# Quarter sums of the weights on GpSimd alone, the single-tile group of the second channel product first, norms of two pairs at a time

## Chip, cores and metric

The kernel runs on one core of a Trainium2 chip. The metric is the device time of one execution in microseconds (us). A trace of one execution is taken by the hardware profiler; its span (first to last instruction) is about 2 us shorter than the time.

Engines: PE is TensorE's matmuls, PEld its weight loads, DVE is VectorE, ACT is ScalarE, POOL is GpSimd, SP is the engine that issues most transfers. "L507" is line 507 of that kernel's source. Lines shift between kernels: L561 of the kernel before is L564 of the changed one.

## The reference

Attention with RMS-normalised q and k, then an MLP-mixer (token mixing, then channel mixing) on its result. There are 8 batches, 12 heads, 448 positions, heads of 64, 768 channels, 256 and 1536 hidden units. All activations are float32; the four mixer weights come as float64.

```python
q_n, k_n = rmsnorm(q, g_q), rmsnorm(k, g_k)          # x / sqrt(mean(x*x) + 1e-6) * g
attn = softmax(q_n @ k_n.T / 8)                      # 448 x 448, per head
x = (attn @ v)                                       # put back to (B, 448, 768)
h = np.maximum(x.T @ w_tok1, 0.0) @ w_tok2           # 448 -> 256 -> 448
u = x + h.T
h2 = np.maximum(u @ w_ch1, 0.0) @ w_ch2              # 768 -> 1536 -> 768
return u + h2
```

## The kernel before

Both channel products are done with seven products of half-size blocks in place of eight (a Strassen scheme), so each needs sums of the weights' quarters. The float64 words of `w_ch1` and `w_ch2` come in as 36 chunks. Each chunk is converted to float32 by VectorE, ScalarE and GpSimd, four sums are made from its four quarters, and the eight blocks are stored to DRAM (`ws1`, `ws2`, `ws3`). PE later loads them back as "units", in every batch.

```python
def combine(j):                              # the four sums of chunk j, and its store
    w, group, m, t = stages[j]
    q = st.pop("stage")
    nc.vector.tensor_tensor(out=q[:, 4], in0=q[:, 1], in1=q[:, 3], op=ALU.add)
    nc.vector.tensor_tensor(out=q[:, 6], in0=q[:, 1], in1=q[:, 0], op=ALU.subtract)
    nc.gpsimd.tensor_tensor(out=q[:, 5], in0=q[:, 4], in1=q[:, 0], op=ALU.subtract)
    nc.gpsimd.tensor_tensor(out=q[:, 7], in0=q[:, 2], in1=q[:, 5], op=ALU.subtract)
    # ... cut: to = the block's place in ws1, ws2 or ws3
    nc.sync.dma_start(out=to.rearrange("q p n -> p q n"), in_=q[:])

def weight_items(lo, hi):                    # three chunks are in work at a time
    def one(i):
        convert_first(i)                     # VectorE: 3 operations
        convert_second(i - 1)                # ScalarE: 2
        convert_last(i - 2)                  # VectorE 1, GpSimd 1, then combine()
        weight_load(i + 2)                   # raw words, on the same queue as the store
```

(Range checks are cut there.) The chunks come in groups: 18 chunks of `w_ch1` (three groups of six), then `w_ch2`'s columns. PE can't use a group of `w_ch2` before all its chunks are stored.

```python
l += [(moe_w_ch2, 3, m, t) for t in range(KF) for m in range(2)]   # "double" group: chunks 19 to 30
l += [(moe_w_ch2, 4, 2, t) for t in range(KF)]                     # "single" group: chunks 31 to 36
```

The norms of a pair of heads: one square on ScalarE, one reduce on VectorE, then eleven small operations on VectorE (mean and epsilon, then the inverse root by three Newton steps). Slices are left out here.

```python
nc.scalar.activation(out=sq, in_=qk, func=AF.Square)
nc.vector.tensor_reduce(out=ms, in_=sq, axis=AX_X, op=ALU.add)
nc.vector.tensor_scalar(ms, ms, 1.0 / D, 1e-6, ALU.mult, ALU.add)
self.rsqrt(rs, ms)                            # ten operations on VectorE
```

A batch's program is a list that is merged with the next batch's attention. It begins with turns (transposes) of x and the first token product, and ends with the two groups of the second channel product and the turns of the result y:

```python
late = [(us(6, HS), lambda i=i, p=p: ch2(b, 0, i, p)) for i in range(7) for p in range(2)]
ys = [0, 1, KC, KC + 1]
for i in range(7):
    late.append((us(6, HS), lambda i=i: ch2(b, 1, i, 0)))
    if i and ys:
        late.append((0.5, lambda cc=ys.pop(0): trans_y(b, cc)))
late += [(0.5, lambda cc=cc: trans_y(b, cc)) for cc in (2, KC + 2)]
```

So four turns of y stand between products, and two stand at the very end, directly ahead of the next batch's three turns of x. I call that place the **seam**.

## Time and profile before

| | before |
|---|---|
| median of the first three runs | 1551.77 us (1550.86 to 1552.11) |
| span of the profiled run | 1550.2 us |
| busy: PE, VectorE, ScalarE, GpSimd | 1415.5, 761.6, 491.9, 468.1 us |
| mean granted TensorE clock | 0.966 |
| first token product of batch 1 | 383.5 us |
| from there to the last batch's first token product | 1039.9 us (five steps of 174.5 us, the last 167.6) |
| from there to the end | 126.8 us |

### The profile page before, as it was taken

The numbers are of one execution on the slowest core, as the hardware profiler recorded it, in microseconds if no ns is written. First come the engines' busy times: TensorE is split into PE (matmuls) and PEld (weight loads), VectorE is DVE, ScalarE is ACT, GpSimd is POOL, SyncE is SP. The second block draws the span as 40 slices with busy tenths as digits, with TensorE's granted clock in tenths as the row PEclk, the third lists the DMA queues.
The fourth block names the chain that finished last, engine by engine and source line by source line (L and its number), as shares of the span: only waits on it lengthen the run. The fifth ranks groups of instructions, "written<-read, shape, count | busy, mean of one in ns | idle before, by whom it ended". The sixth has DMA issues, their size and how long they took to land.

```text
span 1550.2 us, 19250 instructions
## 1 busy us (share of the span) xinstructions
PE 1415.5 (91%) x6976; PEld 1054.6 (68%) x6976; DVE 761.6 (49%) x1513; ACT 491.9 (32%) x850; POOL 468.1 (30%) x424
## 2 busy tenths in 40 slices
PE   5778668477999999999999999999999999999998
PEld 2233445377578857777578857777578857787898
DVE  6977777751454435543454435543454435422321
ACT  5645334311333232323333232323333232312110
POOL 2444455541233213331233213331233213320231
PEclk9989877789999999999999999999999999999999
DMA  5346777676145533446145434446145433444354
GB/s 128 102 138 190 215 207 225 191 242 187 45 140 159 148 87 112 147 132 176 45 140 159 147 87 111 146 131 177 45 140 157 148 88 110 132 125 127 112 166 138
DMA packets 229259, 217.11 MB, mean 140 GB/s; under 512 B 98116, under 2 KB 185668, under 8 KB 229156
## 3 DMA queue, kind: packets, MB, share of 16 engines
q1 hardware_dynamic: 205634, 204.55, 45.8%
q10 hardware_dynamic: 23522, 11.24, 2.7%
q8 instruction: 58, 0.95, 0.3%
q14 instruction: 45, 0.37, 0.1%
HBM read 185.86 MB, written 29.88 MB: 139 GB/s over the span
## 4 chain that ended last, share of the span: by engine, by line
PE 76%; DVE 12%; POOL 3%; issue 3%; ACT 2%; DMA 1%; ACTq 1%; POOLq 0%; SPq 0%; DVEq 0%
PE m_ps L561 24%; PE m_ps L503 22%; PE o_ps L326 8%; PE s_ps L269 8%; PE m_ps L425 5%; PE m_ps L433 4%; POOL stage L212 3%; PE d_ps L340 2%; PE t_ps L404 2%; DVE raw L183 2%; PE t_ps L254 2%; DVE e_t L210 2%; DVE es L316 1%; DVE e_t L182 1%; DVE ms L728 1%
## 5 line engine op out<-in xcount | busy, mean ns | idle before, releaser
L561 PE MATMUL m_ps<-hb,unit 128*128 128x224 f32 x2016 | 402.1, 357 | 30.2 <-DMA unit<-ws 30.2
L561 PEld LDWEIGHTS m_ps<-hb,unit 128*128 128x128 f32 x2016 | 379.9, 192 | 49.8 <-DMA unit<-ws 31.3
L275 ACT ACTIVATE e<-s_ps,rs 112x448 f32<-112x448 f32 x384 | 212.1, 634 | 207.0 <-PE s_ps L269 202.6
L503 PE MATMUL m_ps<-tu,unit 128*128 128x224 f32 x1152 | 238.0, 361 | 12.7 <-DVE hb L508 12.7
L503 PEld LDWEIGHTS m_ps<-tu,unit 128*128 128x128 f32 x1152 | 220.8, 195 | 26.9 <-DVE hb L508 13.1
L269 PE MATMUL s_ps<-qkT 64*112 64x448 f32 x768 | 180.9, 584 | 21.4 <-ACT qkT L256 18.1
L503 PE MATMUL m_ps<-uT,unit 128*128 128x224 f32 x864 | 178.0, 358 | 7.8 <-DVE uT L438 7.8
L503 PEld LDWEIGHTS m_ps<-uT,unit 128*128 128x128 f32 x864 | 161.7, 191 | 26.2 <-issue 11.6
L326 PE MATMUL o_ps<-e,vt 112*64 112x448 f32 x768 | 166.0, 553 | 1.8 <-DVE uT L358 1.8
L570 POOL TENSOR_TENSOR uT<-uT,r 128x448 f32<-128x448 f32 (+1 forms) x64 | 58.4, 923 | 286.3 <-DVE r L570 169.1
L312 POOL TENSOR_TENSOR es<-e 112x896 f32<-112x896 f32 x48 | 100.7, 2098 | 136.3 <-PE d_ps L340 136.3
L269 PEld LDWEIGHTS s_ps<-qkT 64*112 64x112 f32 x768 | 65.5, 181 | 100.0 <-issue 70.4
L316 DVE TENSOR_TENSOR es<-es,e 112x896 f32<-112x896 f32 x96 | 127.8, 1331 | 4.9 <-DVE es L316 0.5
L326 PEld LDWEIGHTS o_ps<-e,vt 112*64 112x64 f32 x768 | 46.7, 136 | 111.8 <-issue 94.3
L570 DVE TENSOR_TENSOR uT<-uT,m_ps 128x448 f32<-128x448 f32 (+1 forms) x80 | 38.8, 502 | 167.6 <-PE m_ps L561 155.3
L256 ACT ACTIVATE qkT<-t_ps,g_t 128x448 f32<-128x448 f32 x96 | 57.7, 631 | 194.3 <-PE t_ps L254 190.9
L352 DVE STREAM_TRANSPOSE dt<-d_ps 128x448 f32<-128x448 f32 x48 | 31.1, 648 | 173.0 <-PE d_ps L340 173.0
L245 POOL TENSOR_TENSOR qk<-qk,rs 112x512 f32<-112x512 f32 x46 | 55.3, 1203 | 197.3 <-ACT e L275 95.0
L425 PE MATMUL m_ps<-x,w_sb 112*128 112x384 f32 x256 | 92.3, 511 | 20.0 <-ACT x L408 12.2
L508 DVE TENSOR_TENSOR r<-m_ps,r 128x448 f32<-128x448 f32 x72 | 44.8, 623 | 123.7 <-PE m_ps L503 82.7
L728 DVE TENSOR_REDUCE ms<-sq 112x16 f32<-112x1024 f32 (+1 forms) x49 | 58.3, 1191 | 62.4 <-ACT sq L725 62.4
L509 ACT ACTIVATE hb<-hb 128x448 f32<-128x448 f32 x72 | 41.5, 577 | 149.1 <-DVE hb L508 117.4
(67 smaller groups left out, 1350.3 us busy)
## 6 DMA issues: line engine op xcount, KB each, us to landing
unit<-ws SPq DMA_DIRECT2D x336, 384.0 KB, 3.2
raw<-in_moe_w_ch_dram SPq DMA_DIRECT2D x72, 256.0 KB, 4.1
ws<-stage SPq DMA_DIRECT2D x36, 512.0 KB, 4.0
vt<-in_v_dram SPq DMA_DIRECT2D x48, 224.0 KB, 2.7
out_dram<-y ACTq DMA_DIRECT2D x48, 224.0 KB, 3.4
qk<-in_q_dram SPq DMA_DIRECT2D x92, 112.0 KB, 3.6
qk<-in_k_dram SPq DMA_DIRECT2D x92, 112.0 KB, 3.8
raw<-in_moe_w_tok_dram SPq DMA_DIRECT2D x4, 448.0 KB, 5.0
```

The source lines that it names most:

```text
L256: nc.scalar.mul(st["qkT", p][:, i, :], ps[:, 0:S], g_t[:, i:i + 1])
L269: nc.tensor.matmul(out=ps[0:R, 0:S], lhsT=qkT[a * D:(a + 1) * D, 1, kc * R:(kc + 1) * R], rhs=qkT[a * D:(a + 1) * D, 0, :], start=True, st ...
L275: nc.scalar.activation(out=e[0:R, a, i, :], in_=pss[a][0:R, 0:S], func=AF.Exp, scale=st["rs", p][0:R, r:r + 1])
L312: nc.gpsimd.tensor_tensor(out=es[0:R], in0=e[0:R, :, 0, :], in1=e[0:R, :, 1, :], op=ALU.add)
L316: nc.vector.tensor_tensor(out=es[0:R], in0=es[0:R], in1=e[0:R, :, i, :], op=ALU.add)
L326: nc.tensor.matmul(out=o[a * D:(a + 1) * D, 0:S], lhsT=vt[0:R, a, kc * D:(kc + 1) * D], rhs=e[0:R, a, i, :], start=(kc == 0), stop=(kc == ...
L425: nc.tensor.matmul(out=ps[:, 0:HC], lhsT=w1_sb[0:R, c, jc * P:(jc + 1) * P], rhs=st["x", h][0:R, c, :], start=(c == 0), stop=(c == NS - 1))
L433: nc.tensor.matmul(out=ps[:, 0:S], lhsT=st["h1", jc][:, cc * P:(cc + 1) * P], rhs=w2_sb[:, jc].rearrange("p c r -> p (c r)"), start=(jc == ...
L503: nc.tensor.matmul(out=ps[:, j * HS:(j + 1) * HS], lhsT=w[:, t, j, :], rhs=m, start=(t == 0), stop=(t == KC - 1))
L561: nc.tensor.matmul(out=ps[:, j * HS:(j + 1) * HS], lhsT=st["w"](j, t), rhs=hb[:, HB[what], t, :], start=(t == 0), stop=(t == KF - 1))
L570: add = lambda e, o, x, y: e.tensor_tensor(out=o, in0=x, in1=y, op=ALU.add)
L728: nc.vector.tensor_reduce(out=ms[0:R, lo * n:hi * n], in_=sq[0:R, lo:hi].rearrange("p i n d -> p (i n) d"), axis=AX_X, op=ALU.add)
```

## The change

Its intent: VectorE waits for GpSimd's multiply before it can make two of the four sums, so all four go to GpSimd (**A**, adds). Ten small operations serve two pairs of heads at once, and the mean and epsilon are folded into an extra column of the reduce and into g (**N**, norms). The single group of `w_ch2` is converted and multiplied first, so that PE's wait after the first channel product needs fewer chunks (**G**, groups). The diff, cut to its core:

```diff
 # A
-        nc.vector.tensor_tensor(out=q[:, 4], in0=q[:, 1], in1=q[:, 3], op=ALU.add)
-        nc.vector.tensor_tensor(out=q[:, 6], in0=q[:, 1], in1=q[:, 0], op=ALU.subtract)
+        nc.gpsimd.tensor_tensor(out=q[:, 4], in0=q[:, 1], in1=q[:, 3], op=ALU.add)
+        nc.gpsimd.tensor_tensor(out=q[:, 6], in0=q[:, 1], in1=q[:, 0], op=ALU.subtract)
 # G
-        l += [(moe_w_ch2, 3, m, t) for t in range(KF) for m in range(2)]
-        l += [(moe_w_ch2, 4, 2, t) for t in range(KF)]
+        l += [(moe_w_ch2, 3, 2, t) for t in range(KF)]
+        l += [(moe_w_ch2, 4, m, t) for t in range(KF) for m in range(2)]
...
+        double = [(us(6, HS), lambda i=i, j=j: ch2(b, 0, i, j)) for i in range(7) for j in range(2)]
+        single = [(us(6, HS), lambda i=i: ch2(b, 1, i, 0)) for i in range(7)]
+        turns = lambda cs: [(0.5, lambda cc=cc: trans_y(b, cc)) for cc in cs]
+        ys = [[0, 1, KC, KC + 1], [2, KC + 2]]
+        second, third = single, double
+        if b == B - 1:
+            second, third = double, single
+            ys.reverse()
+        third = [third[0]] + merge(third[1:-1], turns(ys[1])) + [third[-1]] + turns(ys[0])
+        return items + second, third
...
-            early = merge(early, weight_items(BEFORE, then))
-            late = merge(late[:14], weight_items(then, len(chunks) + 2)) + late[14:]
+            early = merge(early[:-7], weight_items(BEFORE, then)) + merge(
+                early[-7:], weight_items(then, len(chunks) + 2))
 # N
-        if g < NG and h == 0 and p + 2 < NP:
-            items.append((0.0, lambda: pre.norm_pair(p + 2, st)))
-            items.append((0.0, lambda: scale(p + 2)))
+        if g < NG and p % 2 == 0 and p + 2 + h < NP:
+            items.append((0.0, lambda: pre.squares(p + 2 + h, st)))
+            if h == 1:
+                items.append((0.0, lambda: pre.roots(p + 2, 2, st)))
+                items += [(0.0, lambda i=i: scale(p + 2 + i)) for i in range(2)]
...
+        self.sq = const.tile([P, 4 * self.NS, D + 1], F32, name="sq")
+        nc.gpsimd.memset(self.sq[:, :, D:D + 1], D * 1e-6)
```

The four turns of y that need the double group now stand at the end of every batch but the last. And `then`, the chunk at which the first merge ends, follows the first group of `w_ch2`, so 22 in place of 28 of the remaining 34 weight items now run beside the work up to the end of the first channel product. N also issues a pair's loads of q and k one step earlier.

## The prediction

> **What bounds the kernel now.** I read the busy table and slices first, then stretches of time, then waits and order of work.
>
> The stretches show two kernels in one. Columns: from:to, length, then busy us and count for PE, PEld, DVE, ACT, POOL, then granted clock, DMA share, GB/s.
>
> ```profile
> 24.00:118.00 94.00, 71.62 (x312) 28.50 (x311) 77.14 (x171) 52.76 (x90) 38.74 (x30) 0.91 0.39 104
> 118.00:310.00 192.00, 130.41 (x555) 83.33 (x553) 147.63 (x290) 77.86 (x133) 100.14 (x106) 0.83 0.73 207
> 310.00:353.00 43.00, 33.86 (x162) 32.82 (x162) 23.09 (x40) 7.35 (x12) 21.03 (x25) 0.85 0.73 232
> 353.00:384.00 31.00, 23.13 (x124) 21.68 (x123) 4.64 (x10) 4.44 (x8) 2.85 (x5) 0.89 0.70 209
> ```
> ```profile
> 384.00:1551.00 1167.00, 1146.38 (x5788) 883.02 (x5786) 495.05 (x958) 338.29 (x590) 299.83 (x250) 1.00 0.43 126
> ```
>
> From 384 us on, PE is busy for 1146 of 1167 us: each further batch takes 166 us of TensorE. VectorE time saved there buys nothing. The first 384 us hold the attention of batches 0 and 1, the mixer of batch 0, and the conversion of 36 weight chunks (float64 words to float32, plus quarter sums). There PE is busy for 269 us only (1415.5 less 1146.4), so it has 115 us of holes, so the gain must come from there.
>
> What holds PE up? The groups of VectorE between 24 and 353 us (busy us, mean ns, then idle before and releaser):
>
> ```profile
> L183 DVE SCALAR_TENSOR_TENSOR raw<-raw,e_t 128x512 f32<-128x512 uint32 x36 | 35.9, 997 | 1.2
> L162 DVE TENSOR_TENSOR stage<-stage 128x128 f32<-128x128 f32 x36 | 10.5, 292 | 51.9 <-POOL stage L212 51.9
> L163 DVE TENSOR_TENSOR stage<-stage 128x128 f32<-128x128 f32 x36 | 10.2, 284 | 0.0
> L732 DVE TENSOR_SCALAR ms<-ms 112x16 f32<-112x16 f32 x13 | 6.8, 525 | 0.4
> ```
>
> VectorE is busy for 247.9 of these 329 us and waits another 51.9 us at L162 for GpSimd's multiply L212 (36 waits of 1.44 us). That makes 300 of 329 us: its in-order queue sets this stage. A second thing shows in the order of work:
>
> ```profile
> 218.29 0.68 DVE L210 SCALAR_TENSOR_TENSOR e_t<-raw,e_t 128x512 uint32<-128x512 uint32 x1
> ...
> 222.48 1.24 DVE L185 TENSOR_SCALAR e_t<-raw 128x512 uint32<-128x512 uint32 x1
> 223.40 2.28 POOL L312 TENSOR_TENSOR es<-e 112x896 f32<-112x896 f32 x1
> 223.64 2.59 DVE L210 SCALAR_TENSOR_TENSOR e_t<-raw,e_t 128x512 uint32<-128x512 uint32 x1
> ```
>
> L210 takes 0.68 us alone, but 2.59 us when it starts 0.24 us after a GpSimd add of 2.28 us, ending 0.55 us after it. L185 is stretched to 1.24 us (0.43 alone).
>
> Last, PE waits for stored weights twice after the merged part:
>
> ```profile
> 317.32 21.31 PE L561 MATMUL m_ps<-hb,unit 128*128 128x224 f32 x96 [21.76 <-DMA unit<-ws]
> 340.45 12.75 PE L561 MATMUL m_ps<-hb,unit 128*128 128x224 f32 x66 [1.82 <-DMA unit<-ws]
> 359.81 6.93 PE L561 MATMUL m_ps<-hb,unit 128*128 128x224 f32 x24 [6.60 <-DMA unit<-ws]
> ```
>
> The second channel product needs all of a group's chunks stored. The double group (2 of 3 column tiles) becomes ready with chunk 30 near 310 us, the single group with chunk 36 near 353 us.
>
> **What the Trainium skill says.** "SBUF — State Buffer", section "Who interferes with whom": a VectorE operation in a two-port mode, or with two SBUF inputs, and a GpSimd operation that reads SBUF exclude each other; the second to start blocks until the first is through. The lines above agree (2.59 against 0.68 us). The same section says tensor_reduce doesn't contend; L728 means 1.21 us whatever GpSimd does. "GPSIMD Engine Reference", section "Elementwise — side-by-side cycle accounting", has a GpSimd add at about twice VectorE's time; here it is 455 ns (L164) against 284 ns (L163) for 128x128. So the moved adds are cheap for VectorE and dear for the shared pair.
>
> **The change part by part**, over the stretch from 24 us to the last chunk stored (329 us before).
>
> 1. Adds moved to GpSimd. Out of VectorE: 36 x (0.292 + 0.284) = 20.7 us busy and the 51.9 us of waiting, 72.6 us. Into GpSimd: 72 x 0.455 = 32.8 us, and gaps of 0.09 us. After this, no VectorE instruction waits for L212 itself; only buffers tie them (four raw tiles, three stages).
>
> 2. Norms. Before, per pair: L732, then ten small operations, 11 x 0.21 us (start to start) = 2.3 us, and L732 lies at 525 ns where 170 would do, so 0.35 us of blocking: 2.65 us. After, one series of ten for two pairs, some 0.225 us each by my estimate (16 more columns), plus one blocking of 0.35: 2.6 us per two, 1.3 per pair. Saved: 1.35 us x 13 pairs = 17.5 us. The extra column in the reduce is 1/64 of 1.2 us, nothing. In the 35 later pairs the same saving falls on a VectorE that is under half busy: nothing.
>
> 3. Order of the groups. The instruction order shows the seven single products now merged with the last 12 chunks and batch 1's attention, and the 14 half-products of the double group after everything, with no attention beside. VectorE loses 10.3 us of waiting for double products (L570) in the stretch.
>
> Sum for VectorE: 329 - 72.6 - 17.5 - 10.3 = 229 us. But blocking comes on top. GpSimd is busy 160 us in the stretch; some 14 us of it is blocking itself (L165 means 614 ns, 455 alone). With the moved adds it needs 160 - 14 + 33 + 16 of gaps = 195 us, of which I take 165 us as holding the pair (less the gaps and some 0.07 us of fixed cost in each of 200 operations, an estimate). VectorE holds the pair per chunk for about 0.27 + 0.54 + 0.27 + 0.54 = 1.6 us (each uncontended time less some 0.15 us of fixed cost, an estimate), 40 x 1.6 = 64 us, and 26 adds of es at 0.95 = 25 us, others 6: 95 us. **The shared pair thus needs 260 us.** Before, it was 130 us of GpSimd (160 less blocking and fixed cost) and 106 of VectorE (with L162 and L163), 236 of 329. Two queues that block each other won't fill it; at 92% it takes 283 us. So the last chunk is stored 329 - 283 = 46 us sooner, of which some 10 us arise before 118 us.
>
> 4. Given back. Before, 30.2 us lay between the last store's issue (353.3) and the first product of batch 1 (383.5). After, behind the last store come: 6.5 us to the first unit (as now, 353.3 to 359.8), 168 records at 0.19 to 0.20 us (L561) = 33 us, and six turns back with batch 1's first turns, 5.5 us: 45 to 47 us. Loss: 16 us.
>
> 5. Later batches: PE does the same work. Four turns now stand at each seam in place of two, ScalarE copies them (0.585 us each), and PE already waits 12.2 us in total at the seams for L408. I allow 2 us of loss in sum. The last batch keeps its old order, so the tail stays.
>
> Net: 46 - 16 - 2 = 28 us. 1551.8 - 28 = **1524 us**.
>
> **Rivals.**
> (a) VectorE was the limit and blocking stays as it is. For it: VectorE's waits and work make 300 of 329 us. Then the stretch shrinks by the full 100 us to 229 us, and the time falls to about 1551.8 - 100 + 18 = 1470 us. Against: GpSimd would have to run 195 us of 229 beside operations that exclude it.
> (b) The pair saturates fully and GpSimd drags: stores come late, raw tiles come free late, loads follow late (the DMA queue's raw loads already wait 80.6 us for L212). Stretch 305 us, net gain 6 us: 1546 us.
> (c) DMA becomes the limit. Before, 207 GB/s at share 0.73, so about 285 GB/s full. The dense part after 118 us must move some 49 MB, at least 172 us; I expect it to have 200 us. It doesn't bind, but transfers land later and push towards (b).
> (d) The regrouping only moves the hole: PE's 22 us hole goes away, but a new hole before the double products (6.5 us) and the bare 33 us behind it eat part. That is in the sum.
>
> **Range and chances.** My soft numbers are the pair's filling (92%, give or take 5% of 283, so 14 us) and the bare tail of batch 0 (3 us). That gives 1508 to 1541 for eight in ten. The 2% line is near 1521, just below my centre: faster by over 2% has 0.42, within 2% 0.56. Slower would need the seams or the queue of loads to fail badly: 0.02.
>
> **What will show it.** Right, if: L161 to L164 stand on GpSimd at 0.46 to 0.6 us with no VectorE wait on L211 left; VectorE's L181 to L184 and L209 stretch to a mean above the present 2.9 us per chunk in sum; GpSimd is busy for over 75% of the dense part; the last store is issued near 307 us, the double products follow with one wait of 6 to 12 us, and batch 1 starts near 354 us; after that the period is still 166 us. Wrong towards (a) if conversions keep their 2.9 us and the last store comes before 290 us; towards (b) if VectorE waits for raw loads or GpSimd, and the last store comes after 325 us. If the later period differs from 166 us, step 5 is wrong.

## The result

The changed kernel is slower: median 1589.14 us of four runs (1588.80 to 1589.31) against 1551.32 us of the kernel before in the same rounds; ratio 1.0244, 95% interval 1.0227 to 1.0262. Ratios here and below are the mean time of one kernel's runs over that of the other's of the same rounds, so they are not quite the ratio of the medians that are quoted. Executions over 1.5% slower than the fastest of the same kernel are left out of the means.

First, the same stretches of time. Columns as in the prediction: from:to, length, busy us and count of PE, PEld, DVE, ACT, POOL, granted clock, DMA share, GB/s. The changed kernel:

```profile
260.00:278.00 18.00, 0.29 (x1) 0.33 (x2) 12.05 (x16) 3.94 (x7) 16.39 (x18) 0.62 0.58 166
278.00:322.00 44.00, 32.54 (x141) 24.83 (x141) 23.16 (x38) 16.66 (x28) 28.27 (x40) 0.81 0.82 242
322.00:351.00 29.00, 0.95 (x3) 0.45 (x3) 15.25 (x25) 4.54 (x7) 17.66 (x23) 0.56 0.50 144
351.00:392.00 41.00, 37.99 (x199) 36.33 (x198) 5.65 (x9) 4.63 (x8) 4.48 (x4) 0.92 0.62 182
```

PE has two holes, of 18 and 28 us, where it does next to nothing while GpSimd and VectorE finish chunks. The order of work on PE names what ends them (start, busy us, operation; in brackets the idle time before and its releaser):

```profile
184.46 4.81 PE L507 MATMUL m_ps<-uT,unit 128*128 128x224 f32 x12 [11.12 <-DMA unit<-ws]
...
229.83 4.31 PE L507 MATMUL m_ps<-uT,unit 128*128 128x224 f32 x12 [16.66 <-DMA unit<-ws]
...
277.70 6.54 PE L564 MATMUL m_ps<-hb,unit 128*128 128x224 f32 x24 [17.96 <-DMA unit<-ws]
...
350.55 11.07 PE L564 MATMUL m_ps<-hb,unit 128*128 128x224 f32 x42 [28.05 <-DMA unit<-ws]
```

Every one is a wait for a group to be stored and loaded back. With small ones they make 75 us (in the changed kernel's page: 46.0 at L564, 27.8 and 1.6 at L507), against 30.2 us before. The last store is issued at 344.2 us (before: 353.3), and batch 1's first token product starts at 391.9 us (before: 383.5).

Next, the groups of VectorE and GpSimd up to 390 us (busy us, mean ns of one, then idle before and releasers):

```profile
L181 DVE TENSOR_SCALAR e_t<-raw 128x512 uint32<-128x512 uint32 x36 | 20.7, 575 | 45.4 <-DMA raw<-in_moe_w_ch_dram 26.9 <-POOL stage L161 7.9 <-POOL stage L211 5.1
```
```profile
L211 POOL TENSOR_TENSOR stage<-raw,e_t 128x512 f32<-128x512 f32 x36 | 53.9, 1498 | 60.9 <-DVE e_t L209 50.2 <-issue 8.2 <-ACT r L516 2.4
...
L161 POOL TENSOR_TENSOR stage<-stage 128x128 f32<-128x128 f32 x36 | 22.6, 628 | 2.8
L164 POOL TENSOR_TENSOR stage<-stage 128x128 f32<-128x128 f32 x36 | 19.6, 544 | 2.8
```

VectorE's 51.9 us of waiting for the multiply have gone, as intended. In their place it waits 45.4 us at the *head* of the conversion, most of it for raw words that have not arrived. GpSimd still waits 50.2 us for VectorE (71.0 before, up to 353 us). As I read it, no engine of this loop is full; the loop itself has become the limit. The raw loads are late because of the queue that issues them. Waits of that queue from 118 us on (engine and line, waited for, us in total, times, longest), first before, then after:

```profile
SPq L155 <- POOL stage L212: 71.6, 23, 8.6
SPq L172 <- POOL stage L165: 28.9, 32, 1.5
SPq L172 <- DVE stage L163: 21.1, 9, 3.6
```
```profile
SPq L171 <- POOL stage L164: 79.1, 30, 6.7
SPq L154 <- POOL stage L161: 25.3, 9, 4.5
```

L154 and L155 issue raw loads; L171 and L172 issue the stores. Before, the queue mostly waited for a raw buffer to come free. After, it mostly stands at a store whose sums are not done, and the next raw load stands behind that store.

The rest of the loss lies after 392 us, where the prediction allowed 2 us. The second seam (batch 1 to batch 2) on PE, first before, then after:

```profile
548.66 4.71 PE L561 MATMUL m_ps<-hb,unit 128*128 128x224 f32 x24
...
554.41 1.48 PE L404 MATMUL t_ps<-ident,uT 128*112 128x128 f32 x12
556.24 0.65 PE L404 MATMUL t_ps<-ident,uT 128*112 128x128 f32 x4 [0.35 <-ACT qkT L256]
557.95 2.85 PE L425 MATMUL m_ps<-x,w_sb 112*128 112x384 f32 x8 [1.06 <-ACT x L408]
```
```profile
559.82 3.76 PE L564 MATMUL m_ps<-hb,unit 128*128 128x224 f32 x19
...
567.75 0.65 PE L405 MATMUL t_ps<-ident,uT 128*112 128x128 f32 x4 [0.64 <-ACT y L409]
569.03 0.65 PE L405 MATMUL t_ps<-ident,uT 128*112 128x128 f32 x4 [0.64 <-ACT qkT L255]
571.24 4.51 PE L426 MATMUL m_ps<-x,w_sb 112*128 112x384 f32 x8 [1.56 <-DVE x L411]
```

Between the last channel product and the first token product lie 4.6 us before (548.66 + 4.71 to 557.95) and 7.7 us after. And the *same* eight token products then take 4.51 us rather than 2.85. The stretches show why, before and after:

```profile
555.50:558.00 2.50, 1.09 (x9) 0.60 (x7) 1.37 (x2) 1.69 (x3) 0.00 (x0) 1.00 0.76 206
558.00:560.50 2.50, 2.50 (x8) 1.39 (x8) 0.00 (x0) 0.00 (x0) 0.00 (x0) 1.00 0.81 203
```
```profile
568.50:571.00 2.50, 0.65 (x4) 0.41 (x4) 2.30 (x9) 1.54 (x3) 0.97 (x1) 1.00 1.05 276
571.00:573.50 2.50, 2.26 (x4) 1.35 (x5) 0.09 (x1) 0.00 (x0) 1.07 (x2) 0.58 0.46 123
573.50:576.00 2.50, 2.50 (x7) 1.14 (x7) 0.00 (x0) 0.21 (x1) 0.00 (x0) 0.73 0.00 0
```

The granted clock falls to 0.58 and 0.73 just behind the thin stretch, the one in which PE has little to do. This happens at every seam of the changed kernel: the first eight token products of batches 1 to 6 take 4.51 to 5.49 us, and the last batch's group of sixteen 7.12 (5.43 before).

The loss of 37.0 us of span, by the three cuts: batch 0 +8.4, middle +27.0, tail +1.6. Nearly three quarters of it come where the prediction allowed 2 us. Of the middle's 27.0 us, PE's idle time makes 10.4 (22.8 against 12.4 before). The trace's clock records also show half clock (0.50) for 29.3 us there, against none before; by my estimate that costs half of it, 15 us.

### The profile page after: what moved, and what is told of

Same layout as the page of the kernel before. It is cut to its first block, busy times and chain, and to the rows that moved or that the text cites. A ratio compares the mean times of both kernels' runs of the same rounds, so it can differ in the third digit from the quotient of the medians.

```text
span 1587.2 us, 18958 instructions
## 1 busy us (share of the span) xinstructions
PE 1426.4 (90%) x6976; PEld 1058.7 (67%) x6976; DVE 670.1 (42%) x1162; ACT 492.2 (31%) x850; POOL 508.7 (32%) x497
## 4 chain that ended last, share of the span: by engine, by line
PE 79%; DVE 8%; DMA 5%; POOL 4%; issue 2%; ACT 1%; SPq 1%; ACTq 0%; DVEq 0%; POOLq 0%
PE m_ps L564 24%; PE m_ps L507 23%; PE s_ps L268 9%; PE o_ps L325 8%; PE m_ps L426 6%; PE m_ps L434 4%; DMA raw<-in_moe_w_ch_dram 2%; PE d_ps L339 2%; PE t_ps L253 2%; POOL stage L211 1%; DVE es L315 1%; PE t_ps L405 1%; DVE ms L739 1%; DVE raw L182 1%; DVE e_t L209 1%
## 5 line engine op out<-in xcount | busy, mean ns | idle before, releaser
L564 PE MATMUL m_ps<-hb,unit 128*128 128x224 f32 x2016 | 404.1, 359 | 46.0 <-DMA unit<-ws 46.0
L564 PEld LDWEIGHTS m_ps<-hb,unit 128*128 128x128 f32 x2016 | 382.4, 193 | 71.9 <-issue 41.2
L507 PE MATMUL m_ps<-tu,unit 128*128 128x224 f32 x1152 | 231.0, 354 | 1.6 <-DMA unit<-ws 1.6
L507 PEld LDWEIGHTS m_ps<-tu,unit 128*128 128x128 f32 x1152 | 215.5, 190 | 11.4 <-issue 5.6
L507 PE MATMUL m_ps<-uT,unit 128*128 128x224 f32 x864 | 181.0, 361 | 30.4 <-DMA unit<-ws 27.8
L507 PEld LDWEIGHTS m_ps<-uT,unit 128*128 128x128 f32 x864 | 163.6, 194 | 51.0 <-issue 29.8
L268 PE MATMUL s_ps<-qkT 64*112 64x448 f32 x768 | 177.4, 576 | 13.3 <-ACT qkT L255 11.7
L573 POOL TENSOR_TENSOR uT<-uT,r 128x224 f32<-128x224 f32 (+1 forms) x64 | 62.6, 988 | 259.6 <-DVE r L573 155.1
L573 DVE TENSOR_TENSOR uT<-uT,m_ps 128x224 f32<-128x224 f32 (+1 forms) x80 | 38.9, 502 | 233.6 <-PE m_ps L564 168.0
L426 PE MATMUL m_ps<-x,w_sb 112*128 112x384 f32 x256 | 106.1, 571 | 23.0 <-ACT x L409 12.0
L315 DVE TENSOR_TENSOR es<-es,e 112x896 f32<-112x896 f32 x96 | 117.1, 1220 | 6.9 <-POOL es L311 1.3
L244 POOL TENSOR_TENSOR qk<-qk,rs 112x512 f32<-112x512 f32 x46 | 48.8, 1081 | 178.9 <-DMA out_dram<-y 44.0
L426 PEld LDWEIGHTS m_ps<-x,w_sb 112*128 112x128 f32 x256 | 54.1, 220 | 67.5 <-ACT x L409 23.3
L512 POOL TENSOR_TENSOR hb<-r,r 128x448 f32<-128x448 f32 x24 | 28.5, 1187 | 208.9 <-ACT r L528 208.9
```

The source lines that it names most:

```text
L268: nc.tensor.matmul(out=ps[0:R, 0:S], lhsT=qkT[a * D:(a + 1) * D, 1, kc * R:(kc + 1) * R], rhs=qkT[a * D:(a + 1) * D, 0, :], start=True, st ...
L315: nc.vector.tensor_tensor(out=es[0:R], in0=es[0:R], in1=e[0:R, :, i, :], op=ALU.add)
L426: nc.tensor.matmul(out=ps[:, 0:HC], lhsT=w1_sb[0:R, c, jc * P:(jc + 1) * P], rhs=st["x", h][0:R, c, :], start=(c == 0), stop=(c == NS - 1))
L507: nc.tensor.matmul(out=ps[:, j * HS:(j + 1) * HS], lhsT=w[:, t, j, :], rhs=m, start=(t == 0), stop=(t == KC - 1))
L512: add = lambda e, o, x, y: e.tensor_tensor(out=o, in0=x, in1=y, op=ALU.add)
L564: nc.tensor.matmul(out=ps[:, j * HS:(j + 1) * HS], lhsT=st["w"](j, t), rhs=hb[:, HB[what], t, :], start=(t == 0), stop=(t == KF - 1))
```

## The experiments

Fifteen kernels ran. This table has all of them by the three cuts, as differences of the profiled run from the kernel before (383.5, 1039.9, 126.8 us). The ratio is against the kernel before.

| kernel | median us | ratio (95%) | batch 0 | middle | tail |
|---|---|---|---|---|---|
| changed (A + N + G) | 1589.14 | 1.0244 (1.0227 to 1.0262) | +8.4 | +27.0 | +1.6 |
| no_regroup (A + N) | 1550.30 | 0.9987 (0.9970 to 1.0004) | −11.3 | +10.6 | +0.1 |
| regroup_only (G) | 1586.63 | 1.0225 (1.0208 to 1.0242) | +8.5 | +23.3 | +2.8 |
| adds_only (A) | 1545.86 | 0.9957 (0.9941 to 0.9974) | −5.7 | 0.0 | −0.5 |
| norms_only (N) | 1555.19 | 1.0020 (1.0003 to 1.0037) | −6.4 | +10.5 | −0.2 |
| seam_old | 1572.71 | 1.0135 (1.0118 to 1.0152) | +8.4 | +10.5 | −0.5 |
| weights_early | 1585.63 | 1.0216 (1.0199 to 1.0233) | +4.5 | +27.4 | +1.2 |
| adds_late | 1541.65 | 0.9932 (0.9915 to 0.9948) | −11.5 | 0.0 | 0.0 |
| loads_first | 1536.67 | 0.9899 (0.9883 to 0.9916) | −15.2 | 0.0 | −0.2 |
| no_adds (wrong result) | 1514.36 | 0.9757 (0.9741 to 0.9773) | −35.9 | 0.0 | −0.5 |
| norms_odd | 1577.13 | 1.0157 (1.0139 to 1.0175) | −8.4 | +33.8 | −0.3 |
| turns_split | 1563.34 | 1.0077 (1.0060 to 1.0094) | +6.9 | +3.9 | −0.2 |
| late_loads_first | 1540.45 | 0.9923 (0.9906 to 0.9939) | −10.5 | 0.0 | −0.5 |
| fold_single | 1532.81 | 0.9876 (0.9860 to 0.9893) | −17.1 | 0.0 | −0.3 |
| pairs_first | 1531.67 | 0.9867 (0.9850 to 0.9883) | −17.8 | 0.0 | −0.1 |
| after_loads | 1582.88 | 1.0200 (1.0183 to 1.0218) | +4.3 | +25.7 | +1.7 |

My theory after the result: G loses at the seams (turns bunched, then the clock) and in the bare tail of batch 0 (from the last store to batch 1, with no attention beside it), and A gains little because of the loop of raw loads, sums and stores. Rivals: the norms' burst (the small operations for two pairs in one step) costs the seams; A alone makes the stores late; the weights merged too late cost batch 0.

### One part at a time: no_regroup, regroup_only, adds_only, norms_only

no_regroup is the changed kernel with the old order of groups:

```diff
-        l += [(moe_w_ch2, 3, 2, t) for t in range(KF)]
-        l += [(moe_w_ch2, 4, m, t) for t in range(KF) for m in range(2)]
+        l += [(moe_w_ch2, 3, m, t) for t in range(KF) for m in range(2)]
+        l += [(moe_w_ch2, 4, 2, t) for t in range(KF)]
```

(with the old `unit_list`, `mlp_items` and merge.)

> Kernel before with the adds on GpSimd and the norms by two pairs, but with the old order of the two groups everywhere. Theory A (the new order is what costs: it lets TensorE run into weights that are not stored yet, and it crowds the seams between batches): faster than before, 1505 to 1530 us, later batches again 166 us apart. Theory B (GpSimd and VectorE exclude each other so much that moving the adds is itself the loss): 1555 us or more.

regroup_only is the kernel before with the G hunks alone:

```diff
-        l += [(moe_w_ch2, 3, m, t) for t in range(KF) for m in range(2)]
-        l += [(moe_w_ch2, 4, 2, t) for t in range(KF)]
+        l += [(moe_w_ch2, 3, 2, t) for t in range(KF)]
+        l += [(moe_w_ch2, 4, m, t) for t in range(KF) for m in range(2)]
```

> Kernel before with the new order of groups alone. Theory A: slower than the changed kernel, 1595 to 1620 us: later batches 170 us apart as in the changed kernel (the seams cost some 27 us over seven), TensorE waiting 70 us or more for units in the first 400 us. Theory B: about as before, 1545 to 1560 us.

adds_only is the kernel before with the A hunk alone:

```diff
-        nc.vector.tensor_tensor(out=q[:, 4], in0=q[:, 1], in1=q[:, 3], op=ALU.add)
-        nc.vector.tensor_tensor(out=q[:, 6], in0=q[:, 1], in1=q[:, 0], op=ALU.subtract)
+        nc.gpsimd.tensor_tensor(out=q[:, 4], in0=q[:, 1], in1=q[:, 3], op=ALU.add)
+        nc.gpsimd.tensor_tensor(out=q[:, 6], in0=q[:, 1], in1=q[:, 0], op=ALU.subtract)
```

> Kernel before with the two adds of each chunk moved to GpSimd alone. Theory A: VectorE loses 72 us of work and waiting, other waits give half of it back: 1510 to 1535 us. Theory B: 1555 us or more.

norms_only is the kernel before with the N hunks alone:

```diff
-            items.append((0.0, lambda: pre.norm_pair(p + 2, st)))
+            items.append((0.0, lambda: pre.squares(p + 2 + h, st)))
+            if h == 1:
+                items.append((0.0, lambda: pre.roots(p + 2, 2, st)))
```

> Kernel before with the norms of two pairs at a time alone. Both theories: 13 pairs lie in the stretch where VectorE is the limit, 1.35 us each, 17 us at most: 1533 to 1545 us. Later batches 166 us apart.

Measured: 1550.30, 1586.63, 1545.86 and 1555.19 us, with 1552.65 us for the kernel before. G alone makes nearly all of the loss. Without it the kernel is as fast as before. A gains about 6 us, all in batch 0. N gains 6.4 us in batch 0 and gives 10.5 us back at the later seams. None of the four landed in a range that I had recorded.

Why N costs the seams is seen in norms_only's VectorE, at the seam whose first token product starts at 552.33 us:

```profile
545.01 2.28 DVE L315 TENSOR_TENSOR es<-es,e 112x896 f32<-112x896 f32 x2
547.20 0.38 DVE L571 TENSOR_TENSOR uT<-uT,m_ps 128x224 f32<-128x224 f32 x1
547.50 1.23 DVE L735 TENSOR_REDUCE ms<-sq 112x16 f32<-112x1040 f32 x1
548.77 0.18 DVE L761 TENSOR_SCALAR rs<-ms 112x32 int32<-112x32 int32 x1
...
550.90 1.28 DVE L411 COPY x<-t_ps 112x512 f32<-112x512 f32 x2
```

Two sums, a reduce and the whole series of ten stand in one step, and VectorE's in-order copy of x (L411) stands behind them. PE's wait for x is then 1.87 us in place of 1.06, and here too the clock falls and eight token products take 4.51 us. The wait alone doesn't decide: one seam each of no_regroup, norms_only and seam_old has the wait of 1.87 us and still 2.82 us for its eight products. The clock records settle why. From 400 to 1500 us the clock of all 17 traces changes only on a grid of 3.41 us, and every stretch of half clock lasts one step of it (28 times) or two (13). Of the steps at full clock, all 38 with PE busy for under 46% were followed by half clock, none of the 5380 with over 56%, and 3 of the 7 between. In norms_only PE is busy for 1.22 us of the step from 549.49 us, and the next step has half clock. At the seam that escapes, the grid cuts the pause otherwise: 1.71 us of the step from 904.47 us are busy, and the clock stays.

adds_only shows how little VectorE gains from losing 20.7 us of work. Its busy time in the first 384 us falls by 1.4 us only (266.6 to 265.2; as that window now reaches 5.7 us further into batch 1, some 2 us more is a fair estimate, at the later share of 495 in 1167 us), since the sums of e stretch from 1323 to 1538 ns (L316, 5.6 us in all) beside the busier GpSimd, and the small operations of the norms (L732 to L744) take 6.9 us more (both up to batch 1). And it waits 23.9 us for raw loads.

### Which part of G: seam_old, weights_early, turns_split

seam_old leaves batch 0 as in the changed kernel and gives later batches the old order:

```diff
-        return l + (double + single if b == B - 1 else single + double)
+        return l + (double + single if b else single + double)
...
-        if b == B - 1:
+        if b:
             second, third = double, single
```

> The changed kernel, but batches 1 to 7 take the groups in the old order (double first, two turns at the seam); batch 0 keeps the new order. Theory A (each seam costs 4 us: four turns copied by ScalarE between TensorE's turns, waits, then the next products at half the clock): the period goes back to 166 us, 1587 - 27 = 1558 to 1564 us. Theory C (the later batches are slower for another cause of the change, such as the norms of two pairs in one burst): the period stays at 170 us, 1583 to 1590 us.

weights_early merges all remaining weight items with the work ahead of the single group:

```diff
-            early = merge(early[:-7], weight_items(BEFORE, then)) + merge(
-                early[-7:], weight_items(then, len(chunks) + 2))
+            early = merge(early[:-7], weight_items(BEFORE, len(chunks) + 2)) + early[-7:]
```

> The changed kernel with all 34 remaining weight chunks of batch 0 merged beside its first part, so that the seven single products no longer share a part with the last 12 chunks. Theory A (the new order hands the chunks out too thinly before the products that need them, so that TensorE waits for stored units): the waits of the first channel product for units, 29 us in the changed kernel, fall under 5 us, and the total wait for units from 76 us to under 40 us; 1565 to 1578 us, with the 27 us of the seams still in. Theory D (the wait only moves, the chunks take their 6 us each whatever the order): 1583 to 1592 us.

turns_split starts from regroup_only and puts two of the four turns between the last two products, in all batches but the last:

```diff
-        third = [third[0]] + merge(third[1:-1], turns(ys[1])) + [third[-1]] + turns(ys[0])
+        if b == B - 1:
+            third = [third[0]] + merge(third[1:-1], turns(ys[1])) + [third[-1]] + turns(ys[0])
+        else:
+            third = ([third[0]] + merge(third[1:-1], turns(ys[1])) + turns(ys[0][:2]) + [third[-1]]
+                     + turns(ys[0][2:]))
```

> The run with the new order alone (1587 us), with the turns of the first two tiles moved in between the last two products of a batch, so that only two turns stand at the seam, as in the kernel before; batch 0 is as in that run but for its last turns. Theory A (four turns in a row at the seam, with ScalarE's copies, make the pause): period from 178 and 179.4 back to 174.5 to 176 us, 1562 to 1572 us. Rival (the longer products at the end, or the order of loads, make the pause): above 1580 us.

seam_old: 1572.71 us (the kernel before: 1552.14). Its middle is +10.5 us, just the norms' part, and batch 0 is unchanged at +8.4. So the new order in batches 1 to 7, bunched turns included, costs 16.5 us in the middle and 2.1 us in the tail on top of the norms. The total lies between my two recorded ranges, since both causes are at work.

turns_split: 1563.34 us against regroup_only's 1586.63, in theory A's range. Two turns moved by one product bring back 23 us, of which 22 lie at the seams and in the tail: the middle goes from +23.3 to +3.9 and the tail from +2.8 to −0.2. Its second seam:

```profile
562.01 1.48 PE L404 MATMUL t_ps<-ident,uT 128*112 128x128 f32 x12
563.76 0.65 PE L404 MATMUL t_ps<-ident,uT 128*112 128x128 f32 x4 [0.27 <-ACT qkT L256]
565.47 2.85 PE L425 MATMUL m_ps<-x,w_sb 112*128 112x384 f32 x8 [1.07 <-ACT x L408]
```

The wait is back at 1.07 us and the products at 2.85 us. No step from 400 to 1500 us has half clock. This is the direct proof for the seams: no work was taken away, only the bunch.

weights_early: 1585.63 us, as the rival (theory D) had it. PE's waits for groups shrink to 5.8 us, all in the first channel product, yet batch 1 starts only 3.9 us sooner than in the changed kernel. The last store is issued at 333.6 us, 10.6 us sooner, but now nearly all 21 products of the second channel part, and the turns, lie behind it (54.4 us, 333.6 to 388.0). The holes only moved: up to batch 1 PE is idle for 109.9 us (130.7 in the changed kernel), of which it now waits 34.7 us for ScalarE's copies qkT (15.6) and 23.7 us for its exponentials e (11.5). And the stores still end 27 us later than the 307 us I predicted.

### What limits the gain of A: adds_late, loads_first, late_loads_first, no_adds

adds_late leaves the sums where they were before, but makes them one chunk later, so that VectorE need not wait for the multiply:

```diff
-        q = st.pop("stage")
+        q = st.pop(("stage", j))
...
-            combine(i - len(first))
+            j = i - len(first)
+            st["stage", j] = st.pop("stage")
+            done = j + 1 if j + 1 in stage_end else j
+            for k in range(st.get("stored", 0), done):
+                combine(k)
```

> The kernel before with the adds left on VectorE, but each issued one chunk later, so that VectorE has no wait for GpSimd's multiply and GpSimd has no more work. Theory E (in the run with the adds alone the gain went into blocking between VectorE and GpSimd): 52 us of VectorE's wait go without more blocking, 1515 to 1535 us. Theory F (it went into waits for raw loads and into TensorE, ScalarE and VectorE waiting in turn): 1540 to 1550 us, as with the adds on GpSimd (1546 us).

loads_first is adds_only with the next raw load issued before the chunk's sums and store:

```diff
-        if i >= len(first):
-            combine(i - len(first))
...
                 weight_load(i + 2)
+            if len(first) <= i - 2:
+                combine(i - 2 - len(first))
```

> The run with the adds alone (1546 us), where the queue of SyncE now issues the next raw load before the store of the chunk and not behind it. Theory F: VectorE's 24 us of waiting for raw loads fall under 8 us and the time to 1525 to 1538 us. Theory E: the waits turn into blocking, 1542 to 1548 us.

late_loads_first does the same to adds_late:

```diff
-            done = j + 1 if j + 1 in stage_end else j
-            for k in range(st.get("stored", 0), done):
-                combine(k)
...
                 weight_load(i + 2)
+            j = i - 2 - len(first)
+            if j >= 0:
+                for k in range(st.get("stored", 0), j + 1 if j + 1 in stage_end else j):
+                    combine(k)
```

> Adds on VectorE one chunk later (1542 us), and the raw load issued before the store, as in the run with loads first (1537 us). If the two gains are of different waits: 1530 to 1537 us. If GpSimd's added work did not matter beside the loads: 1536 to 1542 us.

no_adds makes no sums at all and stores the four quarters twice, so that as many bytes are stored. Its result is wrong (relative error 0.99):

```diff
-        nc.vector.tensor_tensor(out=q[:, 4], in0=q[:, 1], in1=q[:, 3], op=ALU.add)
-        nc.vector.tensor_tensor(out=q[:, 6], in0=q[:, 1], in1=q[:, 0], op=ALU.subtract)
-        nc.gpsimd.tensor_tensor(out=q[:, 5], in0=q[:, 4], in1=q[:, 0], op=ALU.subtract)
-        nc.gpsimd.tensor_tensor(out=q[:, 7], in0=q[:, 2], in1=q[:, 5], op=ALU.subtract)
...
+        for k in range(2):
+            nc.sync.dma_start(out=to[4 * k:4 * k + 4].rearrange("q p n -> p q n"), in_=q[:, 0:4])
```

> Wrong result on purpose: the kernel before without any of the four quarter sums of a chunk, on either engine; the store writes the four quarters twice, so the transfers keep their bytes. It shows the most that freeing VectorE and the shared pair of this work can give. Theory E (VectorE and the pair set the first stretch): 100 us of work and waiting go, 1490 to 1515 us. Theory F (other waits, above all TensorE's wait for a whole stored group, stand just behind): 1525 to 1540 us, no better than the kernel with loads first (1537 us).

Measured: 1541.65, 1536.67, 1540.45 and 1514.36 us; the first two as theory F had it, no_adds at the upper edge of theory E's range. The ceiling is 37 us: I take it that nothing done to the sums can gain more in this order. Moving them to GpSimd gains 6 us of it, delaying them on VectorE 10, moving them and loading first 15. VectorE's group at the head of the conversion, first in adds_only, then in loads_first:

```profile
L182 DVE TENSOR_SCALAR e_t<-raw 128x512 uint32<-128x512 uint32 x36 | 21.7, 604 | 32.5 <-DMA raw<-in_moe_w_ch_dram 23.9 <-POOL stage L212 3.1 <-POOL stage L163 2.5
```
```profile
L182 DVE TENSOR_SCALAR e_t<-raw 128x512 uint32<-128x512 uint32 x36 | 20.0, 557 | 15.2 <-POOL stage L212 7.3 <-DMA raw<-in_moe_w_ch_dram 5.5 <-POOL stage L163 2.4
```

The wait for raw loads falls from 23.9 to 5.5 us, and batch 0 becomes 9.5 us shorter (from −5.7 to −15.2). So the queue's order, not the speed of the transfers, held the loads. In late_loads_first the same edit gains nothing (1540.45 against 1541.65 us, in different calls). In adds_late VectorE waits only 6.9 us for raw loads, so there is little to win. What costs there, as I read the trace, is blocking. VectorE's busy time in the first 384 us goes *up*, from 266.6 to 285.8 us, with the same instructions (some 5 us of it may be the 11.5 us more of batch 1 in that window). The second sum, L163, takes 655 ns in the mean; it took 284 ns in the kernel before, where none of the 36 met a GpSimd operation that was already running (12 of 36 do in adds_late). That alone is 36 x 0.371 = 13.4 us.

### Where to put the norms' series: norms_odd, fold_single, pairs_first

norms_odd moves the series of two pairs to steps of odd pairs, away from the seam:

```diff
-        if g < NG and p % 2 == 0 and p + 2 + h < NP:
+        if g < NG and (p % 2 == 1 or g == 0) and p + 2 + h < NP:
             items.append((0.0, lambda: pre.squares(p + 2 + h, st)))
-            if h == 1:
-                items.append((0.0, lambda: pre.roots(p + 2, 2, st)))
+            n = 2 if h == 1 else 1 if p in (0, NP - 3) else 0
+            if n:
+                items.append((0.0, lambda: pre.roots(p + 3 + h - n, n, st)))
```

> The run with the norms alone (1555 us), with the pairs grouped 3+4, 5+6 and so on in place of 2+3, 4+5, so that the long series of VectorE no longer stands at the seam between batches. Theory A' (the norms lost 10.6 us because at each seam the series delays VectorE's copy for the first token product, and the pause drops TensorE's clock): period back from 175.2 and 177 to 174.5 us, the 6.4 us gained in batch 0 stay, 1542 to 1548 us. Rival (the burst costs anywhere): 1553 to 1557 us.

This missed my expectation. The seams are mended (1.06 us of wait, 2.85 us for the products, as before), but the kernel is slower still: 1577.13 us, middle +33.8. From 375 us on:

```profile
L505 PE MATMUL m_ps<-uT,unit 128*128 128x224 f32 x756 | 165.3, 371 | 18.8 <-DVE uT L440 18.8
```

The kernel before has no wait in that group after 384 us, and a mean of 355 ns. The wait is 18.8 us, and 756 matmuls at 16 ns more make 12 us: together 31 of the 33.8 us. The burst now stands ahead of VectorE's sums after the second token product (L440), which PE waits for. One such place, columns as in the other stretches:

```profile
405.00:407.50 2.50, 0.59 (x3) 0.01 (x1) 2.23 (x11) 0.00 (x0) 0.45 (x1) 1.00 0.57 129
407.50:410.15 2.65, 1.02 (x4) 0.67 (x4) 2.62 (x4) 0.00 (x0) 2.65 (x4) 1.00 0.00 0
410.15:413.30 3.15, 3.15 (x10) 2.37 (x10) 1.53 (x3) 0.00 (x0) 1.97 (x3) 0.54 0.02 5
```

VectorE is full with the ten small operations (404.69 to 406.9 us) and what follows, PE stands thin for 5 us, and then the granted clock is 0.54: the same pattern as at the seam, at another place. My theory that the seam was the only tender place fell; the burst is dear where PE depends on VectorE at short notice.

fold_single therefore drops it: old groups, adds on GpSimd, loads first, and the folded constant, but one pair a step:

```diff
-        if g < NG and p % 2 == 0 and p + 2 + h < NP:
-            items.append((0.0, lambda: pre.squares(p + 2 + h, st)))
-            if h == 1:
-                items.append((0.0, lambda: pre.roots(p + 2, 2, st)))
-                items += [(0.0, lambda i=i: scale(p + 2 + i)) for i in range(2)]
+        if g < NG and h == 0 and p + 2 < NP:
+            items.append((0.0, lambda: pre.squares(p + 2, st)))
+            items.append((0.0, lambda: pre.roots(p + 2, 1, st)))
+            items.append((0.0, lambda: scale(p + 2)))
```

(against no_regroup; the loads as in loads_first.)

> Old order, adds on GpSimd, raw loads before stores, and the norms without the scaling operation, but one pair a step as before. If the burst of two pairs was the cause at the seams: later batches 174.5 us apart, batch 1 starts at 364 to 368 us, 1531 to 1536 us. If the series as such was: 1540 us or more.

pairs_first takes two pairs at a time only in the first twelve pairs, where VectorE matters:

```diff
+    PAIRED = 2 * NPAIR
...
+        if g < NG and p < PAIRED and p % 2 == 0 and p + 2 + h < NP:
+            items.append((0.0, lambda: pre.squares(p + 2 + h, st)))
+            if h == 1:
+                items.append((0.0, lambda: pre.roots(p + 2, 2, st)))
```

> As fold_single, with two pairs at a time for the pairs of batches 0 and 1 only, where VectorE is pressed. If the burst only costs at later seams: batch 1 starts some 3 us earlier still, 361 to 366 us, later batches 174.5 us apart, 1528 to 1534 us. If the two-pair burst gains nothing in batch 0 beyond the fold: as fold_single.

1532.81 and 1531.67 us, four runs each, with 1552.16 us for the kernel before; both are correct. The middle is back to the period of before in both, with N's earlier loads of q and k still in, so the burst was what N cost. pairs_first is the fastest kernel of this study, 1.3% below the kernel before and 3.6% below the changed one (1531.67 over 1589.14, from different calls). It can't be told from fold_single, whose interval overlaps; two pairs at a time in batch 0 are worth at most about a microsecond there.

### The remaining question on batch 0: after_loads

The changed kernel with the loads ahead of the stores, its groups in the new order:

```diff
-        if i >= len(first):
-            combine(i - len(first))
...
                 weight_load(i + 2)
+            if len(first) <= i - 2:
+                combine(i - 2 - len(first))
```

> The changed kernel with the raw load issued before the store. If the raw loads were what held its chunks back: batch 1 starts at 378 to 384 us in place of 392, total 1574 to 1580 us. If TensorE's waits for stored groups set its first batch: batch 1 at 388 us or later, 1583 to 1589 us.

1582.88 us, just under my second range and some 6 us below the changed kernel (1589.14, from another call), batch 0 at +4.3. The last store is issued at 341.2 us, only 3 us sooner; in the old order the same edit brought it 8.6 us nearer (346.8 to 338.2). PE still waits 20.8 us for the single group and 22.7 and 4.0 us for the double one. So the queue's order explains a part of batch 0, not the most of it.

## Why the prediction was wrong, point by point

**Step 5 failed most: seams, "2 us of loss in sum".** Measured: 27.0 us in the middle and 1.6 in the tail. I saw the four turns and the wait for x, and allowed 2 us for them, but nothing for the lower clock behind them, which by the estimate above is the larger part (15 us against 10.4 of idle time). turns_split and fold_single show two causes by taking them away: bunched turns (22 us in middle and tail by themselves) and the norms' burst (10.5 us by itself). They don't add: together with what else the order costs they make 28.6. I also took the norms' saving in later pairs as "nothing"; it is a loss.

**The period was mis-sized,** here and in the expectations that speak of 166 or 170 us. I divided 1167 us by seven and wrote 166 us. The last of the seven batches has no attention beside it and takes 127 us. The true step was 174.5 us, and the changed kernel's is 178.4 to 179.8 (the last step 171.3).

**Steps 1 and 3 and the sum failed: the stretch of the chunks.** Predicted: the last store near 307 us. Measured: 344.2. The term of waiting at L162 was right and went away, but I booked it as a gain. It turned into 45.4 us at L181, because other things close the loop. Raw loads behind stores are shown by loads_first; GpSimd's longer chain (four adds at 539 to 628 ns and a multiply at 1498 ns, 3.75 us a chunk) and PE's order of groups are argued. I wrote that "only buffers tie" VectorE to GpSimd, and gave the buffers no cost. no_adds bounds what could have been had from A: 36 us in batch 0 with *no* sums at all. Moving them was worth 5.7. In the prediction's own sum, 46 − 16 − 2 = 28 us became 9.1 − 17.5 − 28.6 = −37.0 us. The 260 us of the shared pair rest on fixed costs of 0.07 and 0.15 us that I gave without a source, and no run measured how full the pair was.

**Step 2: the size per series was right, its worth was not.** One series of ten for two pairs starts an operation every 0.22 us (0.225 estimated). But 17.5 us of VectorE became 6.4 us at batch 1. VectorE wasn't the limit that I took it for.

**Step 4 held.** The bare tail of batch 0 is 47.7 us (45 to 47 predicted, 30.2 before). With the last store 9.1 us sooner and the bare tail 17.5 longer, batch 0 becomes 8.4 us longer. That alone made the regrouping a bad trade in batch 0.

**The rivals.** (b) was nearest for the store's time (after 325 us, VectorE waiting for raw loads), but its 1546 us kept the same 2 us for the seams; the 80.6 us of waits that I gave for it are 82.0 us in the trace. (d) was right in kind: the hole moved and grew, from 30.2 to 75 us of waits for units. (a) is refuted. (c) is not supported: DMA share was 0.50 to 0.82 in the dense stretches, and loads_first gained without moving fewer bytes.

**Signs I had named.** Conversions did not stretch: VectorE's four per chunk sum to 2.92 us (2.9 before). GpSimd was busy for 70% of 118 to 351 us, not 75. The adds on GpSimd fell in or slightly above the range of 0.46 to 0.6 us.

**What stays open.** A, N and G each bring the last store, or batch 1, some 6 to 8 us nearer when tried alone; together the last store gains only 9.1 us. Groups stored later relative to PE's order (22 items beside the first part in place of 28), raw loads behind stores, and the shared pair all take part, and weights_early and after_loads each change one and gain 4 us. How the rest divides wasn't separated.

## What to carry to other kernels

In a stretch where PE is 98% busy, look at the few places where it isn't, and count what a change puts into them: a run of short operations whose copies outlast them costs its waits *and*, where it left PE busy for less than about half of a 3.41 us step, a lower clock behind them. Spread such operations between long ones (turns_split: 23 us for moving two turns). When a wait is removed from a loop of engines, buffers and one in-order queue, name the next wait in that loop before booking a gain, and issue the loads that feed the loop ahead of the stores that end it.

## What the Trainium skill lacked or had wrong

- "TensorE: Matmul & The Clock Gate", section "Part 1: The HAM clock gate": it ties the low clock to an idle window of about 3.4 us, and doesn't say how much work still counts as idle. Here single waits of 1.56 to 1.87 us were enough, if PE was busy for under 46% of a step of 3.41 us (38 of 38); over 56%, the clock never fell. The section "A second HAM failure mode: psum-queue depth-cycling" does tell of frequent short idles that lower the clock, which fits, but gives no size or threshold. The page puts the penalty of a warm-up below 1% of a typical span; my estimate of 15 us for the middle of the changed kernel is 0.9% of its span, which agrees, but the waits come on top.
- "SBUF — State Buffer", section "Who interferes with whom": it agrees with the single cases, but gives no way to size them in a mix. With 20.7 us of adds taken from VectorE, its busy time in the first 384 us fell by 1.4 us (adds_only), and with sums only made one chunk later it rose by 19.2 us (adds_late; 13.4 of it at one add, 284 to 655 ns).
- "GPSIMD Engine Reference", section "Elementwise — side-by-side cycle accounting": its factor of about two is for 2048 elements. At 128 the runs show 455 against 284 ns, 1.6, and 539 to 628 ns once VectorE is busy beside it.
- "Perfetto Trace Analysis", section "DMA Instruction — HWDGE (DVE, Sync)", has the issuing sequencer wait for an instruction's semaphores before it uses the descriptor generator, and the traces agree (79.1 us in which the stores of L171 wait for L164). It doesn't say what follows: a store that waits holds the loads behind it. Issuing the load first cut VectorE's wait for loads from 23.9 to 5.5 us.
